# A weight exchange on TensorE, half of the v loads on another engine's queue, and a new order on GpSimd, in a windowed attention and gated convolution kernel

## The chip, the cores and the metric

The kernel runs on one core of one Trainium2 chip. The metric is the device time of one execution in microseconds (us). A single-core run is called slow here when it lies over 1.5% above the fastest run of the same kernel; the comparisons of times below use the other, fast, runs.

## The reference

There are 8 batches, 8 heads, 576 positions and 64 channels per head. Heads 0 to 3 see a plain window of 32 positions, heads 4 to 7 a window dilated by 4. The output of the attention, 512 channels wide, is the input of a causal gated convolution unit.

```python
def _attn_ref(q, k, v):
    window, dilation, scale = 32, 4, 1.0 / np.sqrt(D)
    scores = scale * np.matmul(q, k.transpose(0, 1, 3, 2))
    mask_plain = (rel >= 0) & (rel < window)
    mask_dil = (rel >= 0) & (rel < window * dilation) & (rel % dilation == 0)
    ...                                   # masked softmax over the keys
    return np.matmul(attn, v)

def _moe_ref(x, w_val, conv_w, w_out):
    for k in range(5):
        gate_pre += conv_w[k] * xp[:, k:k + S, :]      # causal, per channel
    gate = 1.0 / (1.0 + np.exp(-gate_pre))
    return (gate * (x @ w_val)) @ w_out
```

## The kernel before

The work is cut into 32 iterations: four per batch, each of two heads (128 channels). Iterations 0 and 1 of a batch are plain heads, 2 and 3 dilated ones. A *group* `g` is four heads of a batch, so group 2b is the plain half of batch b and group 2b + 1 the dilated one. The names that matter:

- `k_nat`, `q_nat`, `qk_rest`: loaded k and q; `k_b`, `q_b`: the same converted to bf16 for plain heads.
- `vPst`, `v_st`: loaded plain and dilated v; `vP`, `vA`: converted by GpSimd. `vPst` has two halves: partitions 0 to 63 (z = 0) and 64 to 127 (z = 1, the "upper half"), each with a load of its own.
- `w_out_b`: the output weights. Output tiles of one parity read them as they are, the others read `w_out_s`, in which the two halves of 64 rows are exchanged.

```python
def load_v(g, a=0, e=4, eng=nc.sync):
    ...
    if not dil:
        per = NB // 2
        dst = vPst[b % NVP]
        for z in range(2):
            ...
            eng.dma_start(out=dst[D * z:D * z + D, first:e * per, :], in_=...)

def swap_out():                       # the exchange of the halves, by DMA
    for h in range(2):
        nc.gpsimd.dma_start(out=w_out_s[D * h:D * h + D], in_=w_out_b[D - D * h:2 * D - D * h])

# (cut) before the loop
    make_mask_d()
    make_perm()
    prep_v(0)                         # GpSimd: v of iteration 0 to bf16
    for i in range(NP):
        # (cut) loads of the groups ahead, all on SyncE's queue
        if i + 1 < NP:
            prep_v(i + 1)
        # (cut) early k/q conversions
        if i == 3:
            load_weight(w_out_b, moe_w_out)
        if i == 5:
            swap_out()
        g2 = g + 2
        if 2 < g2 < 2 * B and g2 % 2 == 0:
            cast(g2, "k" if a == 0 else "q", 0, nc.gpsimd)
            cast(g2, "k" if a == 0 else "q", 2, nc.gpsimd)
        scores(i, 0)                  # TensorE, then exp on ScalarE
        scores(i, 1)
        if i == 0:
            cast(0, "k", 2, nc.scalar)
            cast(0, "q", 2, nc.scalar)
        run_conv(i - 1)               # TensorE, then the gate on ScalarE
        # (cut) masks, transposes of the next pair
        attn_v(i, 0)                  # attention products, read vP or vA
        attn_v(i, 1)
        normalize(i)
        # (cut) the value products and output tiles of the batch before
```

The softmax here doesn't subtract the row's maximum and nothing guards it: scores larger than these inputs give would overflow.

Of the kernel before, what the change touches and what calls it, by code (L numbers as in the profile page):

```python
# [23 lines left out]
def kernel(  # L24
# [47 lines left out]


    ident = consts.tile([128, 128], BF16, name="ident")
    perm = consts.tile([96, 96], BF16, name="perm")
    ident5 = consts.tile([8, 8], FP32, name="ident5")
    mask_p = consts.tile([128, NB, 96], BF16, name="mask_p")
# [27 lines left out]
    def bank():  # L105
        return ps_one.tile([128, 512], FP32, name="ps_bank")
# [16 lines left out]
    def load_rest(g, name, eng):  # L123
# [14 lines left out]
        else:  # L138
# [2 lines left out]
                in_=bass.AP(tensor=src.tensor, offset=off,  # L141
                            ap=[[2 * D, 2 * TR], [S * D, 4], [1, 2 * D]]))

    def load_v(g, a=0, e=4, eng=nc.sync):
        b, dil = g // 2, g % 2
        t = grp_tiles.setdefault(g, {})
        if not dil:


            per = NB // 2  # L150
            dst = vPst[b % NVP]
            for z in range(2):
                first = a * per
                if b == 0 and a == 0 and z == 0:
                    eng.dma_start(
                        out=dst[16:D, 0, :],
                        in_=v[0, 0, 0:96, :].rearrange("(p j) d -> p (j d)", j=2))
                    first = 1
                eng.dma_start(
                    out=dst[D * z:D * z + D, first:e * per, :],  # L160
                    in_=bass.AP(
                        tensor=v.tensor,
                        offset=v.offset + (b * H * S + 192 * first + 96 * z - 32) * D,
                        ap=[[2 * D, D], [192 * D, e * per - first], [1, 2 * D]]))
        else:
            if "vst" not in t:
                t["vst"] = vst_pool.tile([128, 4, DIL * D], FP32, name="v_st")
                t["vBst"] = vst_pool.tile([128, 4, 2, D], FP32, name="vB_st")
            eng.dma_start(
                out=t["vst"][:, a:e, :],  # L170
                in_=v[b, 4 + a:4 + e, 0:RM, :].rearrange("h (p r) d -> p h (r d)", r=DIL))
            eng.dma_start(
                out=t["vBst"][:, a:e].rearrange("p h j d -> p h (j d)"),
                in_=v[b, 4 + a:4 + e, DIL * TB:S, :].rearrange("h (p j) d -> p h (j d)", j=2))
# [8 lines left out]
    def cast(g, name, a, eng):  # L183

        t = grp_tiles[g]
        if name + "b" not in t:
            t[name + "b"] = qb_pool.tile([128, DIL, 4, D], BF16, name=f"{name}_b")
        dst = t[name + "b"][:, :, a:a + 2, :]
        src = t[name][:, a:a + 2, :].rearrange("p h (r d) -> p r h d", r=DIL)
        if eng is nc.scalar:  # L190
            nc.scalar.copy(out=dst, in_=src)
        else:
            eng.tensor_copy(dst, src)  # L193

    def prep_v(i):
        b, c, dil, g, a = pair_info(i)
        t = grp_tiles[g]
        e = a + 2
        if not dil:
            nc.gpsimd.tensor_copy(  # L200
                vPs[b % NVP][:, a:e, :, 0:D],
                vPst[b % NVP][:, a * NB // 2:e * NB // 2, :].rearrange(
                    "p (h u) (j d) -> p h (u j) d", u=NB // 2, j=2))
        else:
            nc.gpsimd.tensor_copy(
                vAs[b % NVD][:, a:e, :, 0:D],
                t["vst"][:, a:e, :].rearrange("p h (r d) -> p h r d", r=DIL))
            nc.gpsimd.tensor_copy(
                vBs[b % NVD][:, a:e, :, 0:D], t["vBst"][:, a:e, :, :])
# [6 lines left out]
    def load_pair(g, a):  # L216
        load_main(g, "k", a, a + 2, nc.sync)
        load_main(g, "q", a, a + 2, nc.sync)
        if a == 0:
            load_rest(g, "k", nc.sync)  # L220
            load_rest(g, "q", nc.sync)
        load_v(g, a, a + 2)
# [5 lines left out]
    load_rest(0, "k", nc.sync)  # L228
    load_rest(0, "q", nc.scalar)
    load_v(0, 0, 2)  # L230
    nc.scalar.dma_start(out=conv_nat, in_=moe_conv_w)
    nc.scalar.activation(out=warm_in, in_=warm_in, func=AF.Exp, scale=1.0)
    load_main(0, "k", 2, 4, nc.sync)
    load_main(0, "q", 2, 4, nc.sync)
    load_v(0, 2, 4)
    load_pair(1, 0)
    load_pair(1, 2)
    nc.vector.memset(junk, 1.0)
# [5 lines left out]
        base=0, pattern=[[-1, 128]], channel_multiplier=1,  # L244
    )
    nc.vector.tensor_tensor(out=ident_h, in0=ident[:, 0:D], in1=ident[:, D:2 * D], op=ALU.add)
    nc.gpsimd.memset(ident5, 0.0)
    nc.gpsimd.affine_select(
        out=ident5, in_=ident5, compare_op=ALU.not_equal, fill=1.0,
# [50 lines left out]
    def make_mask_d():  # L300
        band(mask_d[:, 0:TM], [[1, TM]], 0)
        nc.gpsimd.tensor_copy(mask_d[:, TM:2 * TM], mask_d[:, 0:TM])

        mb = mask_d[:, 2 * TM:HB].rearrange("p (w t) -> p w t", w=2)
        nc.gpsimd.memset(mb, 1.0)
        for (lo, up) in ((True, 0), (False, 0)):
            sg = 1 if lo else -1
            base = 2 * (TM - TB) if lo else 2 * (window - 1) - 2 * (TM - TB)
            nc.gpsimd.affine_select(
                out=mb, in_=mb, compare_op=ALU.is_ge, fill=0.0, base=base,  # L310
                pattern=[[sg, 2], [2 * sg, TR]], channel_multiplier=-sg)
        nc.gpsimd.iota(par_i, pattern=[[1, 2]], base=1, channel_multiplier=1)
# [19 lines left out]
    def make_conv_diag(c):  # L332
        nc.vector.tensor_tensor(
            out=conv_diag[:, c, :, :],
            in0=ident_h[:, None, :].to_broadcast([128, K, D]),
            in1=conv_w_sb[:, c, :, None].to_broadcast([128, K, D]),
            op=ALU.mult)

    def swap_val():
        x, y = (w.rearrange("p m (c h d) -> p (m c) h d", h=2, d=D) for w in (w_val_b, w_val_s))  # L340
        for h in range(2):
            nc.gpsimd.tensor_copy(y[:, :, h, :], x[:, :, 1 - h, :])

    def swap_out():
        for h in range(2):
            nc.gpsimd.dma_start(out=w_out_s[D * h:D * h + D], in_=w_out_b[D - D * h:2 * D - D * h])

    def load_weight(dst, src):
        nc.gpsimd.dma_start(out=dst, in_=src.rearrange("(c p) n -> p c n", p=128))
# [315 lines left out]
    setup_conv_w()  # L665
    make_conv_diag(0)
    make_conv_diag(1)
    make_mask_d()
    make_perm()
    prep_v(0)  # L670
    for i in range(NP):
        b, c, dil, g, a = pair_info(i)
        if i == 0:
            load_pair(2, 0)
        elif i == 1:
            load_pair(2, 2)
        elif i == 2:
            load_pair(3, 0)
        elif i == 3:
            load_pair(3, 2)  # L680
            load_group(4)
        if c % 2 == 0 and 5 <= g + 3 < 2 * B:
            load_group(g + 3)
        if i + 1 < NP:
            prep_v(i + 1)
        if i == 1:
            load_weight(w_val_b, moe_w_val)
        if i == 2:
            for name in ("k", "q"):
                cast(2, name, 0, nc.gpsimd)  # L690
        if i == 3:
            load_weight(w_out_b, moe_w_out)
            for name in ("k", "q"):
                cast(2, name, 2, nc.gpsimd)
        if i == 4:
            swap_val()
        if i == 5:
            swap_out()
        g2 = g + 2
        if 2 < g2 < 2 * B and g2 % 2 == 0:  # L700
            cast(g2, "k" if a == 0 else "q", 0, nc.gpsimd)
            cast(g2, "k" if a == 0 else "q", 2, nc.gpsimd)
        scores(i, 0)
        scores(i, 1)
        if i == 0:
            cast(0, "k", 2, nc.scalar)
            cast(0, "q", 2, nc.scalar)
        run_conv(i - 1)
        apply_mask(i, 0)
        if i > 0:  # L710
            after_x(i - 1)
        if 1 < i < NCH:
            next_pair(i)
        if i >= EARLY and g + 1 < 2 * B:
            trans_main(g + 1, "k" if a == 0 else "q")
        apply_mask(i, 1)
        if 0 < i < 3:
            make_conv_diag(i + 1)
        if i < NCH:
            warm(3 if i == 0 else 2)  # L720
        elif c == 0 and outs:
            run_out()
        elif vals:
            run_val()
        attn_v(i, 0)
        attn_v(i, 1)
        normalize(i)
        if i == 1 or NCH <= i < EARLY:
            next_pair(i)
        if i == EARLY - 1:  # L730
            trans_main(g + 1, "k")
        if i == 0:
            next_pair(0)
            finish_mask_d()
        elif i >= EARLY - 1 and a == 0 and g + 1 < 2 * B:
            trans_rest(g + 1)
        if i < NCH - 1:
            warm(2)
        if c == 0 and vals:
            run_val()  # L740
        for _ in range((2 if len(outs) > 2 else 1) - (c == 0 and i > NCH)):
            if outs:
                run_out()
        if vals:
            run_val()
# [39 lines left out]
```

## Time and profile before

| | kernel before |
|---|---|
| time, median of the runs beside the changed kernel | 183.33 us (182.02 to 184.41, 4 runs) |
| span of the profiled execution | 183.2 us (that run took 185.49 us as a whole, 2 us above the median and 1.9% above the fastest run, so slow by the rule above; its granted clock, 0.963, is like that of the fast ones) |
| TensorE busy | 87% of the span |
| longest wait of TensorE | 5.2 us, for `w_out_s` |

The views are read in the prediction below: the page's busy times and slices, the chain of work that ended last, the stretches around the hole. One more view of the kernel before is needed later, ScalarE's timeline in iteration 0. The columns of an engine's timeline are the start, the busy time, engine, line, operation, output and input; in brackets stands the idle time ahead of it and what ended it.

```profile
7.05 1.19 ACT L456 ACTIVATE et<-ps_sc 128x576 bf16<-128x576 f32 x2 [0.85 <-PE ps_sc L436]
8.13 0.62 ACT L191 CAST k_b<-k_nat 128x512 bf16<-128x512 f32 x1
9.48 0.62 ACT L191 CAST q_b<-q_nat 128x512 bf16<-128x512 f32 x1 [0.73 <-DMA q_nat<-in_q_dram]
```

After the two exponentials ScalarE converts k at 8.13 us and q at 9.48 us. TensorE needs both to go on to iteration 1.

### The profile page before, as it was taken

To read this page: it belongs to the slowest core of one execution; us is meant where nothing else is said; L and a number is where in the kernel's file an instruction comes from. 1 tells how busy PE (TensorE), PEld (TensorE's weight loads), DVE (VectorE), ACT (ScalarE), POOL (GpSimd) and SP (SyncE) were. 2 spreads that over 40 slices of the span, in tenths; PEclk is the share of its full clock that TensorE was granted. 3 is DMA by queue.
4 is the path that set the end of the run, shared out by engine and by line. 5 is a ranking of instruction groups with operands and counts; after the bars stand their busy time and mean duration, and the time that the engine had idled before them with its cause. 6 is when DMAs were issued, how large, how long until landed. Compare 5 with 4: busy or idle time off the path is not lost.

```text
span 183.2 us, 6768 instructions
## 1 busy us (share of the span) xinstructions
PE 158.7 (87%) x2799; PEld 108.8 (59%) x2827; DVE 120.2 (66%) x292; ACT 115.9 (63%) x217; POOL 59.2 (32%) x118
## 2 busy tenths in 40 slices
PE   6768878979259999999996999999999999999990
PEld 2445556656137667667774776777677767665540
DVE  4647667855404988688775766976797869773320
ACT  3625764759227677777874788778877786564440
POOL 7857166065302730850093028300750400000000
PEclk9957999999957999999999999999999999999999
DMA  5999999999999999999999999999999322224354
GB/s 149 249 300 326 236 263 260 357 197 193 206 338 245 214 319 362 231 334 334 291 222 300 296 291 221 307 309 290 185 333 343 106 61 61 61 57 106 104 166 145
DMA packets 51688, 42.91 MB, mean 234 GB/s; under 512 B 6997, under 2 KB 46917, under 8 KB 51658
## 3 DMA queue, kind: packets, MB, share of 16 engines
q1 hardware_dynamic: 49888, 40.57, 84.1%
q0 software_dynamic: 1216, 1.57, 4.9%
q8 instruction: 22, 0.36, 0.9%
q10 hardware_dynamic: 554, 0.34, 0.6%
q14 instruction: 8, 0.07, 0.1%
HBM read 33.56 MB, written 9.44 MB: 235 GB/s over the span
## 4 chain that ended last, share of the span: by engine, by line
PE 72%; DVE 7%; POOL 6%; DMA 6%; issue 4%; ACT 2%; POOLq 0%; ACTq 0%
PE ps_bank L599 17%; PE ps_bank L583 14%; PE ps_bank L566 12%; PE ps_bank L365 7%; DMA w_out_s<-w_out_b 6%; PE ps_sc L479 5%; PE ps_sc L436 3%; PE ps_sc L493 3%; PE ps_sc L453 3%; DVE et L465 3%; PE ps_bank L520 3%; PE ps_bank L533 2%; DVE xn L508 2%; PE ps_bank L527 2%; DVE xT L535 1%
## 5 line engine op out<-in xcount | busy, mean ns | idle before, releaser
L456 ACT ACTIVATE et<-ps_sc 128x576 bf16<-128x576 f32 x64 | 38.5, 648 | 13.8 <-PE ps_sc L436 9.9
L604 ACT ACTIVATE osb<-ps_bank 128x512 f32<-128x512 f32 x36 | 21.9, 608 | 32.7 <-PE ps_bank L599 26.1
L589 DVE SCALAR_TENSOR_TENSOR y<-gate,ps_bank 128x288 bf16<-128x288 bf16 x64 | 28.3, 450 | 11.8 <-PE ps_bank L583 9.6
L508 DVE TENSOR_TENSOR xn<-ps_sc,rec 96x768 bf16<-96x768 f32 (+1 forms) x32 | 30.6, 955 | 1.1
L566 PE MATMUL ps_bank<-xT,conv_diag 64*64 64x288 bf16 (+1 forms) x768 | 27.9, 270 | 0.0
L193 POOL CAST k_b<-k_nat 128x512 bf16<-128x512 f32 x14 | 9.2, 679 | 53.9 <-DMA k_nat<-in_k_dram 18.5
L465 DVE TENSOR_TENSOR et<-et,mask_p 128x576 bf16<-128x576 bf16 x32 | 17.4, 547 | 10.8 <-ACT et L456 10.8
L575 ACT ACTIVATE gate<-ps_bank 128x288 bf16<-128x288 f32 x64 | 23.0, 422 | 2.0 <-PE ps_bank L566 1.7
L599 PE MATMUL ps_bank<-w_out_s,y 128*128 128x512 bf16 x59 | 18.4, 394 | 6.1 <-DMA w_out_s<-w_out_b 5.2
L599 PEld LDWEIGHTS <-y 128*128 128x128 bf16 x144 | 12.8, 99 | 17.3 <-issue 6.6
L566 PEld LDWEIGHTS <-conv_diag 64*64 64x64 bf16 x768 | 19.3, 108 | 3.0 <-DVE qB L420 1.0
L583 PE MATMUL ps_bank<-xT,w_val_s 128*128 128x288 bf16 x128 | 20.7, 285 | 0.0
L583 PE MATMUL ps_bank<-xT,w_val_b 128*128 128x288 bf16 x128 | 19.9, 286 | 0.4 <-DVE xT L535 0.4
L465 DVE TENSOR_TENSOR et<-et,mask_d 128x576 bf16<-128x576 bf16 x32 | 15.5, 486 | 6.6 <-ACT et L456 6.4
L535 DVE COPY xT<-ps_bank 128x576 bf16<-128x576 bf16 x32 | 14.6, 456 | 7.4 <-PE ps_bank L533 4.4
L200 POOL CAST vP<-vPst 128x768 bf16<-128x768 f32 x16 | 13.1, 841 | 18.5 <-DMA vPst<-in_v_dram 16.7
L599 PE MATMUL ps_bank<-w_out_b,y 128*128 128x512 bf16 x58 | 17.7, 379 | 0.7
L503 DVE RECIPROCAL rec<-ps_sc 96x12 f32<-96x12 f32 (+1 forms) x32 | 7.4, 231 | 13.8 <-PE ps_sc L479 11.1
L583 PEld LDWEIGHTS <-w_val_s 128*128 128x128 bf16 x128 | 12.1, 97 | 5.6
L479 PE MATMUL ps_sc<-vP,et 64*128 64x65 bf16 x384 | 10.2, 197 | 5.4 <-POOL vP L200 2.9
L479 PEld LDWEIGHTS <-et 64*128 64x128 bf16 x384 | 7.7, 98 | 12.0 <-issue 5.7
L583 PEld LDWEIGHTS <-w_val_b 128*128 128x128 bf16 x128 | 11.7, 98 | 3.6 <-issue 0.2
(93 smaller groups left out, 239.2 us busy)
## 6 DMA issues: line engine op xcount, KB each, us to landing
k_nat<-in_k_dram SPq DMA_DIRECT2D x12, 512.0 KB, 6.5
q_nat<-in_q_dram SPq DMA_DIRECT2D x12, 512.0 KB, 8.0
vPst<-in_v_dram SPq DMA_DIRECT2D x12, 384.0 KB, 8.4
v_st<-in_v_dram SPq DMA_DIRECT2D x6, 512.0 KB, 6.4
k_nat<-in_k_dram SPq DMA_DIRECT2D x8, 256.0 KB, 4.5
out_dram<-osb SPq DMA_DIRECT2D x8, 256.0 KB, 6.4
q_nat<-in_q_dram SPq DMA_DIRECT2D x7, 256.0 KB, 5.0
out_dram<-osb SPq DMA_DIRECT2D x8, 224.0 KB, 5.2
```

The source lines that it names most:

```text
L200: nc.gpsimd.tensor_copy(vPs[b % NVP][:, a:e, :, 0:D], vPst[b % NVP][:, a * NB // 2:e * NB // 2, :].rearrange("p (h u) (j d) -> p h (u j) d ...
L456: nc.scalar.activation(out=e3, in_=ps[:, :, 0:HB], func=AF.Exp, scale=scale)
L465: nc.vector.tensor_tensor(out=e3, in0=e3, in1=m, op=ALU.mult)
L479: nc.tensor.matmul(out=ps[:, z, x * AVS:x * AVS + D + 1], lhsT=et[D * z:D * z + D, h2, col:col + 128], rhs=vPs[b % NVP][D * z:D * z + D, a ...
L508: nc.vector.tensor_tensor(out=dst, in0=av[:, :, :, 0:D], in1=rec[0:R, :, :, None].to_broadcast([R, 2, 6, D]), op=ALU.mult)
L535: nc.vector.tensor_copy(xTs[b % NXT][:, c, :, 2:], pr)
L566: nc.tensor.matmul(out=pss[G][D * hp:D * hp + D, o * T:(o + n) * T], lhsT=conv_diag[D * h:D * h + D, c, K - 1 - m, :], rhs=xt[D * h:D * h ...
L575: nc.scalar.activation(out=gate, in_=pss[G][:, 0:HB], func=AF.Tanh, scale=0.5)
L583: nc.tensor.matmul(out=ps[:, 0:HB], lhsT=w[:, mc, c * 128:(c + 1) * 128], rhs=xt[:, mc, 2 * G:2 * G + 2, 2:], start=(mc == 0), stop=(mc == ...
L589: nc.vector.scalar_tensor_tensor(out=y_half[G][:, c, b * HB:(b + 1) * HB], in0=gates.pop((b, c, G)), scalar=1.0, in1=ps[:, 0:HB], op0=ALU. ...
L599: nc.tensor.matmul(out=ps, lhsT=y_half[G][:, c, 128 * n:128 * n + 128], rhs=w[:, c, :], start=(c == 0), stop=(c == NCH - 1),)
L604: nc.scalar.mul(out=osb, in_=ps, mul=0.5)
```

## The change

The intent is to end two waits of TensorE and to shorten the loads' way. **One**: the exchanged weights are made by TensorE, as a product with an exchanged identity matrix, instead of by two copies that take over 10 us. **Two**: the upper half of plain v is issued by ScalarE, so that SyncE has fewer issues to make and v arrives sooner. **Three**: GpSimd converts v of iteration 0 ahead of making the masks, and around iterations 4 to 6 v ahead of q and k; from iteration 8 on it is the other way round.

```diff
+    ident_x = consts.tile([128, 128], BF16, name="ident_x")   # identity, halves exchanged
@@ load_v: the loop over z becomes a function of its own
+    def load_v_half(g, z, a, e, eng): ...
     def load_v(g, a=0, e=4, eng=nc.sync):
         if not dil:
-            for z in range(2): ...
+            load_v_half(g, 0, a, e, eng)
@@ ahead of the loop
     load_v(0, 0, 2)
+    load_v_half(0, 1, 0, 2, nc.scalar)
     ...
     load_v(0, 2, 4)
+    load_v_half(0, 1, 2, 4, nc.scalar)
@@
-    def swap_out():
-        for h in range(2):
-            nc.gpsimd.dma_start(out=w_out_s[D * h:D * h + D], in_=w_out_b[D - D * h:2 * D - D * h])
+    def swap_out(m, eng):
+        ps = bank()
+        nc.tensor.matmul(out=ps, lhsT=ident_x, rhs=w_out_b[:, m, :], start=True, stop=True)
+        ...                                   # evicted by ScalarE (three) and VectorE (one)
@@
+    prep_v(0)
     make_mask_d()
     make_perm()
-    prep_v(0)
@@ in the loop
-        if i + 1 < NP:
+        if i < 4:
             prep_v(i + 1)
         if i == 4:
             swap_val()
+            prep_v(5)
+            prep_v(6)
+        g2 = g + 2
         if i == 5:
-            swap_out()
-        g2 = g + 2
-        if 2 < g2 < 2 * B and g2 % 2 == 0:
+            prep_v(7)
+            for z in (0, 2):
+                cast(4, "k", z, nc.gpsimd)
+        elif i == 6:
+            for z in (0, 2):
+                cast(4, "q", z, nc.gpsimd)
+        elif 4 < g2 < 2 * B and g2 % 2 == 0:
             cast(g2, "k" if a == 0 else "q", 0, nc.gpsimd)
             cast(g2, "k" if a == 0 else "q", 2, nc.gpsimd)
+        if 7 <= i < NP - 1:
+            prep_v(i + 1)
         scores(i, 0)
         scores(i, 1)
+        if i == 0:
+            load_v_half(2, 1, 0, 2, nc.scalar)
+        elif i == 1:
+            load_v_half(2, 1, 2, 4, nc.scalar)
+        elif i == 3:
+            load_v_half(4, 1, 0, 4, nc.scalar)
+        elif c % 2 == 0 and 5 <= g + 3 < 2 * B and (g + 3) % 2 == 0:
+            load_v_half(g + 3, 1, 0, 4, nc.scalar)
         if i == 0:
             cast(0, "k", 2, nc.scalar)
             cast(0, "q", 2, nc.scalar)
@@ in iteration 5, around normalize(i)
+            swap_out(0, nc.scalar); swap_out(1, nc.scalar)
+            swap_out(2, nc.scalar); swap_out(3, nc.vector)
```

More of the change, by code (lines that the diff above doesn't have):

```diff
@@ L142, in load_rest, with load_v_half @@
                             ap=[[2 * D, 2 * TR], [S * D, 4], [1, 2 * D]]))
+    def load_v_half(g, z, a, e, eng):
+        b, per = g // 2, NB // 2
+        first, dst = a * per, vPst[b % NVP]
+        if b == 0 and a == 0 and z == 0:
+            eng.dma_start(
+                out=dst[16:D, 0, :],
+                in_=v[0, 0, 0:96, :].rearrange("(p j) d -> p (j d)", j=2))
+            first = 1
+        eng.dma_start(
+            out=dst[D * z:D * z + D, first:e * per, :],
+            in_=bass.AP(
+                tensor=v.tensor,
+                offset=v.offset + (b * H * S + 192 * first + 96 * z - 32) * D,
+                ap=[[2 * D, D], [192 * D, e * per - first], [1, 2 * D]]))
     def load_v(g, a=0, e=4, eng=nc.sync):
@@ L147, in load_v @@
         if not dil:
-            per = NB // 2
-            dst = vPst[b % NVP]
-            for z in range(2):
-                first = a * per
-                if b == 0 and a == 0 and z == 0:
-                    eng.dma_start(
-                        out=dst[16:D, 0, :],
-                        in_=v[0, 0, 0:96, :].rearrange("(p j) d -> p (j d)", j=2))
-                    first = 1
-                eng.dma_start(
-                    out=dst[D * z:D * z + D, first:e * per, :],
-                    in_=bass.AP(
-                        tensor=v.tensor,
-                        offset=v.offset + (b * H * S + 192 * first + 96 * z - 32) * D,
-                        ap=[[2 * D, D], [192 * D, e * per - first], [1, 2 * D]]))
+            load_v_half(g, 0, a, e, eng)
         else:
@@ L246 @@
     nc.vector.tensor_tensor(out=ident_h, in0=ident[:, 0:D], in1=ident[:, D:2 * D], op=ALU.add)
+    for h in range(2):
+        nc.vector.tensor_copy(ident_x[:, D * h:D * h + D], ident[:, D - D * h:2 * D - D * h])
     nc.gpsimd.memset(ident5, 0.0)
@@ L342, in swap_val @@
             nc.gpsimd.tensor_copy(y[:, :, h, :], x[:, :, 1 - h, :])
-    def swap_out():
-        for h in range(2):
-            nc.gpsimd.dma_start(out=w_out_s[D * h:D * h + D], in_=w_out_b[D - D * h:2 * D - D * h])
+    def swap_out(m, eng):
+        ps = bank()
+        nc.tensor.matmul(out=ps, lhsT=ident_x, rhs=w_out_b[:, m, :], start=True, stop=True)
+        if eng is nc.scalar:
+            nc.scalar.copy(out=w_out_s[:, m, :], in_=ps)
+        else:
+            eng.tensor_copy(w_out_s[:, m, :], ps)
     def load_weight(dst, src):
@@ L726 @@
         attn_v(i, 1)
+        if i == 5:
+            swap_out(0, nc.scalar)
+            swap_out(1, nc.scalar)
         normalize(i)
+        if i == 5:
+            swap_out(2, nc.scalar)
+            swap_out(3, nc.vector)
         if i == 1 or NCH <= i < EARLY:
```

## The prediction

> **What bounds the kernel now.** I read the page first, its slices and the chain of work that ended last:
>
> ```profile
> PE 158.7 (87%) x2799; PEld 108.8 (59%) x2827; DVE 120.2 (66%) x292; ACT 115.9 (63%) x217; POOL 59.2 (32%) x118
> ...
> PE   6768878979259999999996999999999999999990
> ...
> PEclk9957999999957999999999999999999999999999
> DMA  5999999999999999999999999999999322224354
> ...
> PE 72%; DVE 7%; POOL 6%; DMA 6%; issue 4%; ACT 2%; POOLq 0%; ACTq 0%
> ```
>
> One slice is 4.58 us. From slice 12 on (55 us) TensorE is full to the end, so there it sets the time; the DMA engines are full until slice 30 (142 us). Before that TensorE has one hole, in slices 10 and 11, and its granted clock is low just after it. The same chain in order of time, then the stretches around the hole (columns: stretch, busy us of PE, PEld, DVE, ACT, POOL, clock, DMA share, GB/s):
>
> ```profile
> 38.19 1.27 POOL k_b L193 x2
> 39.46 0.78 POOL vA L205
> 40.59 0.48 POOL w_out_s L346
> 41.06 10.91 DMA w_out_s<-w_out_b
> 52.11 0.58 PE ps_bank L599
> ```
>
> ```profile
> 41.00:46.80 5.80, 5.36 (x93) 4.07 (x90) 3.71 (x10) 5.27 (x10) 2.65 (x6) 1.00 1.13 191
> 46.80:52.10 5.30, 0.11 (x4) 0.02 (x1) 1.34 (x3) 0.29 (x1) 1.60 (x2) 0.85 1.11 242
> 52.10:58.20 6.10, 5.82 (x68) 3.56 (x70) 1.28 (x3) 3.15 (x6) 0.00 (x0) 0.57 1.12 318
> ```
>
> GpSimd works in order. Its k conversion waits for k of group 4 until 38.19, the copies that make the half-exchanged w_out stand behind it, they go out at 40.54 and land about 10.6 us later, and the first output tile that reads them stops TensorE for 5.2 us (46.8 to 52.1) and leaves it at a clock of 0.57 for 6 us. A smaller hole is at the start: the first attention product waits 2.94 us for vP, because GpSimd makes mask_d and perm (6.93 to 10.03) before that conversion.
>
> **What the Trainium skill says.** "TensorE: Matmul & The Clock Gate", Part 1 (the HAM clock gate): TensorE falls to half rate after an idle window of about 3.4 us and needs about as long again to recover. The trace agrees in kind: 0.57 after 5.2 us idle, and 0.50 in 10 to 15 us after the 2.94 us wait. "DMA: Bandwidth & Descriptors", Issuing engines are not separate DMA queues: queues of different engines share the 16 DMA engines, so a second queue saves only issue time. The trace agrees: the v halves cost SyncE 0.64 us of issue each, while the DMA share is over 1.0 in every stretch from 5 to 100 us. Same page, Queues, rings and completion order: each DMA engine takes turns between queues. So a v half on the ScalarE queue goes past what waits on SyncE's queue; no run shows it yet. "Trainium Kernel Development and Optimization", Key Constraints: GpSimd cannot access PSUM; hence the four exchanged blocks must leave PSUM by ScalarE and VectorE, as the diff has them.
>
> **Part by part.**
> (1) Exchange on TensorE. Removed: two copies of 256 KB, the wait of 5.2 us, and the slow clock behind it. Size of the latter: from the first score product of iteration 8 to its attention product took 53.90 to 58.22 = 4.32 us; the same stretch of iteration 12 at full clock took 72.95 to 75.83 = 2.88. That is 1.4; the output tile before it (52.11 to 53.90 = 1.79, against 0.9 at 71.50 to 72.36) gives 0.9. Together 5.2 + 2.3 = **7.5 us** if nothing else stops TensorE. The copies' DMA work goes too: 23.6% of 11.2 us = 2.6 us on their queue (DMA view, 41 to 52.2). Added: four 512-column products at about 0.38 us (row of L599), three ScalarE evictions of 0.6 us (row of L604) and one on VectorE. They stand in iteration 5 (about 34 us), where TensorE next waits for loads (below), so I count 0.
> (2) prep_v(0) ahead of the masks. vP can be made at 7.0 to 7.8 instead of 10.03 to 10.84; the masked scores are ready at 9.03. Gain 10.89 - 9.0 = 1.9 us, and about 1 us of clock. But in iteration 6 the transposes of group 4 need k and q rest rows, whose q part lands at 42.43, and TensorE already waited 0.4 us for it. A start 2 to 3 us earlier only waits longer there: 0 at the end.
> (3) Upper v halves on ScalarE. Packets take 42 to 49 ns each of an engine (queue share x 16 x stretch / packets: 0.908 x 13 us x 16 / 4521 = 42 ns), so a half of 768 packets is 768 x 42 / 16 = 2.0 us of DMA. Issued earlier, it pushes all loads of the SyncE queue behind it back by 2.0 us; against that, SyncE is rid of two issues of 0.64 at the start (1.3 us earlier). Rest q of group 4 then lands at 42.43 + 2.0 - 1.3 = 43.1. ScalarE pays some ten issues of 0.64 us at 63% busy, mostly in its idle time.
> (4) Order on GpSimd. In iterations 4 to 6 v goes ahead of k/q, which ends a 1.31 us wait for vA at 39 us (hidden by the wait at 43.1). But from iteration 8 on the diff puts the k/q conversions **ahead** of prep_v(i + 1); before they came after it:
>
> ```profile
> 47.13 1.60 POOL L200 CAST vP<-vPst 128x768 bf16<-128x768 f32 x2 [3.48 <-DMA vPst<-in_v_dram]
> 58.43 1.17 POOL L193 CAST k_b<-k_nat 128x512 bf16<-128x512 f32 x2 [9.70 <-PE ps_bank L599]
> ```
>
> ```profile
> 62.51 0.63 PE L479 MATMUL ps_sc<-vP,et 64*128 64x65 bf16 x24
> ```
>
> The vP of iteration 9 was made at 47.9. Now it waits for k of group 6, which landed at 58.23 (issued 49.03, 9.2 us). In the new kernel that is 58.23 - 2.6 (copies gone) + 2.0 (the v half of group 6 now ahead) - 1.3 = 56.3; plus two k casts 1.2 and one vP 0.83: vP ready at 58.3. TensorE would want it at 46.8 + 0.65 (rest q) + 10.4 (52.11 to 62.51) - 2.3 (clock) = 55.5. So it waits 2.8 us and starts iteration 9 at 58.3 instead of 62.5: **4.2 us** is left of 7.5. Check of the next gates, with the landing times of before: vA of iteration 10 behind the q cast, ready 59.7 + 2.2 = 61.9, wanted at 66.64 - 4.2 = 62.4: fits. Iteration 13: k landed 74.08, vP at 76.5, wanted at 80.12 - 4.2 = 75.9, but k lands about 1.9 earlier: fits. Iteration 17: 93.6 against 97.75 - 4.2 = 93.5: just fits. Behind that TensorE is full to the end, so the gain stays.
>
> Sum: 183.4 - 4.2 = 179.2; I say **179.0 us**, as the gate at 58.3 is the shakiest number and full gain is larger than no gain is likely.
>
> **The rivals.**
> (a) The GpSimd order costs nothing, because k of group 6 lands by 53.5 or so (two queues being served faster than one, loads of the first 50 us ahead). For: SyncE's queue is backed up there (issues of 1.8 to 2.9 us instead of 0.45), and fewer descriptors stand in it. Against: time per packet hardly changes with queues or sizes. Then the gain is 7 to 7.5: about 176.
> (b) The loads bind more than I think: the v halves delay q of groups 4 and 6 by the full 2.0 and no 1.3 is won, TensorE stands over 3 us in iteration 6 and again in 9, and its clock falls again (1 to 2 us). For: DMA full throughout, and a 2.94 us wait was enough at the start. Gain 1 to 2.5: 181 to 182.4.
> (c) ScalarE becomes the bound, since a DMA issue sits in its order between the exponentials and the gates. For: it is 70 to 80% busy in full stretches. Against: 0.64 us once in four iterations of 4.4 us. At most 1 us in all.
>
> **Range and chances.** The middle is 4.2 gained, (a) gives 7.5 and (b) 1 to 2.5. Range 175.8 to 181.9. 2% is 3.7 us, or 179.8: the middle is only just beyond it. (a) with nearly a third and the upper half of the middle make 0.6 for faster; same 0.37; slower 0.03, since every added cost lies beside waits.
>
> **What would show it.** Right: no wait of an output tile for w_out_s; PEclk full around 50 to 55 us unless a new hole is there; no wait of 2.9 us at the start, yet TensorE near its old time at iteration 6, waiting for qk_rest; in iteration 9 a wait of TensorE on vP of 1.5 to 3 us, right after the k casts of group 6; from there as full as before. Wrong: no wait on vP at iteration 9 (then 176), or waits for vP at iterations 13 and 17 as well, or a clock that falls twice (then over 181); or TensorE well over 1 us ahead of its old times already at iteration 7, which would mean that the loads do not gate there.

## The result, and the profile after

| | before | after |
|---|---|---|
| median of the runs | 183.33 us | 189.8 us (188.77 to 190.41, 4 runs, all fast) |
| ratio | | 1.035, 95% interval 1.026 to 1.044: slower |
| span of the profiled execution | 183.2 us | 187.4 us |

A ratio here and below is the mean time of one kernel's fast runs over that of the other's of the same rounds, so it is not quite the ratio of the medians quoted beside it.

The page of the changed kernel (busy times, the slices of TensorE, its clock and the DMA engines, the chain's shares by engine):

```profile
PE 164.5 (88%) x2831; PEld 110.0 (59%) x2831; DVE 120.6 (64%) x295; ACT 117.0 (62%) x220; POOL 57.3 (31%) x116
...
PE   6536983898999589999999999999999999999990
...
PEclk9855798559999999999999999999999999999997
DMA  5999999999999999688899999989989322123354
...
PE 71%; DMA 15%; DVE 6%; ACT 3%; issue 2%; ACTq 1%; POOL 0%
```

ScalarE's busy time has hardly changed (115.9 to 117.0 us). TensorE's rose by 5.8 us, beside a longer time at half clock: 24 us (7.6 to 21.3 and 31.5 to 41.8), against 14 us before (9.6 to 16.4 and 50.5 to 57.4). And TensorE has new holes in slices 1 to 3 (5 to 19 us) and in slice 6 (28 to 33 us), and the DMA share of the chain went from 6% to 15%. The chain in order of time says where (start, length, what):

```profile
12.21 4.68 DMA v_st<-in_v_dram
...
16.91 9.31 DMA k_nat<-in_k_dram
...
26.23 4.90 DMA v_st<-in_v_dram
...
31.19 0.62 POOL vA L207
31.81 0.04 ACTq L155
...
31.90 0.42 ACT gate L585
...
32.36 0.37 PE ps_bank L410 x2
```

Up to 31 us the chain is one load after another, and from there it goes over a DMA issue on ScalarE (`ACTq L155`, the upper half of v) to a gate and to TensorE. ScalarE's timeline of the changed kernel shows that issue twice, in iteration 0 and in iteration 3:

```profile
8.70 1.19 ACT L466 ACTIVATE et<-ps_sc 128x576 bf16<-128x576 f32 x2 [1.03 <-PE ps_sc L446]
14.19 0.60 ACTq L155 DMA_DIRECT2D vPst<-in_v_dram  x1
14.84 0.62 ACT L193 CAST k_b<-k_nat 128x512 bf16<-128x512 f32 x1 [4.94 <-DMA v_st<-in_v_dram]
```

```profile
27.37 0.65 ACT L466 ACTIVATE et<-ps_sc 128x576 bf16<-128x576 f32 x1 [0.31 <-PE ps_sc L463]
31.23 0.62 ACTq L155 DMA_DIRECT2D vPst<-in_v_dram  x1
31.90 0.71 ACT L585 ACTIVATE gate<-ps_bank 128x288 bf16<-128x288 f32 x2 [3.88 <-POOL vA L207]
```

The issue takes 0.60 us as predicted. But ScalarE is done with its exponentials at 9.89 us and the issue begins at 14.19, 4.3 us later; the k conversion, which stood at 8.13 us before, comes behind it at 14.84. In iteration 3 it is 28.02 to 31.23, 3.2 us. The second releaser is named wrongly: vA of line 207 runs from 31.19 to 31.81, so it cannot release what begins at 31.23.

What does the issue wait for? The program as compiled lists the semaphores. These are lines of ScalarE's program of the changed kernel (the number counts its instructions), and two of SyncE's; the list is not a profile:

```
ScalarE
11 L466 Activation et0_104<-ps_sc_290 128x576 [waits PE_49]
12 L155 DMACopy vPst1_107<-in_v_dram 64x6x128 [waits DMAHW0_49]
13 L193 TensorCopy k_b_220<-k_nat_129 128x4x128
...
31 L155 DMACopy vPst0_106<-in_v_dram 64x12x128 [waits DMAHW4_49,DMAHW3_49,Pool_49]
32 L585 Activation gate_636<-ps_bank_610 128x288 [waits PE_49]
SyncE
12 L171 DMACopy v_st_152<-in_v_dram 128x2x256 [waits DMAHW0_49]
30 L171 DMACopy v_st_473<-in_v_dram 128x2x256 [waits DMAHW4_49]
```

The loads and stores of SyncE's and ScalarE's queues share eight completion semaphores, DMAHW0 to DMAHW7, in rotation over both queues. Each further issue waits until the transfer that had the semaphore before it, eight issues back, has **landed**. For ScalarE's instruction 12 that is SyncE's instruction 12, a `v_st` load. The view of that tile in the changed kernel (its issue, who waited for it, and its time from issue to landing):

```profile
L171 SPq DMA_DIRECT2D v_st<-in_v_dram x1: 592/592/592, 9.3 to 9.3; - x1
...
  ACT k_b L193: 4.9, 1
...
DMA to landing us min/median/max: 4.9/4.9/4.9
```

Issued at 9.27 us, landed 4.9 us later at 14.17; ScalarE's issue begins at 14.19. For iteration 3: issued 26.23, landed 31.13, ScalarE's issue at 31.23. A further issue at 5.92 us waits in the same way for the rest rows of k.

Two statements of the Trainium skill make this worse than it looks. "DMA: Bandwidth & Descriptors", Anatomy of one DMA — SWDGE (gpsimd) path: "any semaphore wait happens on the issuing sequencer before dispatch". It is written of GpSimd's path; the trace agrees for ScalarE's. And "PSUM — Partial Sum Buffer", Engine vs sequencer instructions: the queues of ScalarE, VectorE and GpSimd are strict FIFO, which agrees with the k conversion moving from 8.13 to 14.84 us: its k, issued at 4.59 us, landed 4.2 us later, so it was there by 8.8. SyncE waits in this way as well, but it computes nothing. Behind ScalarE's issue stand the conversions and gates that TensorE needs. TensorE's timeline of the changed kernel:

```profile
10.22 1.02 PE L489 MATMUL ps_sc<-vP,et 64*128 64x65 bf16 x24
15.51 0.61 PE L375 MATMUL ps_bank<-ident,k_b 128*128 128x128 bf16 x4 [4.27 <-ACT k_b L193]
...
32.36 0.37 PE L410 MATMUL ps_bank<-ident,qk_rest 128*128 128x128 bf16 x2 [2.95 <-ACT gate L585]
...
56.82 1.02 PE L609 MATMUL ps_bank<-w_out_s,y 128*128 128x512 bf16 x4
```

A third, earlier wait of 2.14 us belongs to the issue at 5.92 us, which pushed a q conversion from 4.65 to 6.57. The stretches of the changed kernel (columns as in the prediction) show what follows each hole:

```profile
15.50:20.50 5.00, 4.88 (x66) 2.71 (x66) 3.30 (x8) 2.25 (x4) 2.89 (x5) 0.50 1.23 250
29.40:32.40 3.00, 0.05 (x2) 0.04 (x1) 0.00 (x0) 0.50 (x2) 2.24 (x3) 0.86 1.19 227
32.40:40.50 8.10, 7.29 (x106) 5.15 (x106) 4.40 (x12) 3.34 (x8) 1.41 (x3) 0.50 1.14 308
```

The clock is at half in the stretch behind each hole. At the start it had already fallen at 7.6 us, after the wait of 2.14 us and before that of 4.27, and stayed at half until 21.3; the second time it fell at 31.5, within the wait of 2.95 us, and was at half until 41.8. In the last line of TensorE's timeline an output tile on `w_out_s` starts with no wait at all: the wait of 5.2 us is gone, as predicted.

### The profile page after: what moved, and what is told of

It reads as the page before. It is cut to its first block, busy times and chain, and to the rows that moved or that the text cites. A ratio compares the mean times of both kernels' runs of the same rounds, so it can differ in the third digit from the quotient of the medians.

```text
span 187.4 us, 6792 instructions
## 1 busy us (share of the span) xinstructions
PE 164.5 (88%) x2831; PEld 110.0 (59%) x2831; DVE 120.6 (64%) x295; ACT 117.0 (62%) x220; POOL 57.3 (31%) x116
## 4 chain that ended last, share of the span: by engine, by line
PE 71%; DMA 15%; DVE 6%; ACT 3%; issue 2%; ACTq 1%; POOL 0%
PE ps_bank L609 17%; PE ps_bank L593 17%; PE ps_bank L576 12%; DMA k_nat<-in_k_dram 8%; PE ps_bank L375 5%; DMA v_st<-in_v_dram 5%; PE ps_sc L489 4%; PE ps_sc L446 3%; PE ps_sc L463 3%; DMA vPst<-in_v_dram 3%; PE ps_bank L530 3%; PE ps_sc L503 2%; DVE xT L545 2%; PE ps_bank L543 2%; PE ps_bank L537 2%
## 5 line engine op out<-in xcount | busy, mean ns | idle before, releaser
L195 POOL CAST k_b<-k_nat 128x512 bf16<-128x512 f32 x14 | 8.5, 630 | 60.4 <-DMA k_nat<-in_k_dram 25.1
L593 PE MATMUL ps_bank<-xT,w_val_b 128*128 128x288 bf16 x128 | 21.1, 297 | 2.3 <-issue 2.1
L475 DVE TENSOR_TENSOR et<-et,mask_d 128x576 bf16<-128x576 bf16 x32 | 14.9, 466 | 7.0 <-ACT et L466 6.8
L475 DVE TENSOR_TENSOR et<-et,mask_p 128x576 bf16<-128x576 bf16 x32 | 15.7, 493 | 4.7 <-ACT et L466 4.7
L609 PE MATMUL ps_bank<-w_out_b,y 128*128 128x512 bf16 x72 | 18.4, 378 | 0.3
L593 PEld LDWEIGHTS <-w_val_b 128*128 128x128 bf16 x128 | 12.2, 102 | 6.5 <-issue 2.6
L207 POOL CAST vA<-v_st 128x512 bf16<-128x512 f32 x16 | 9.9, 616 | 9.2 <-DMA v_st<-in_v_dram 9.2
```

Of the source, the lines that this page charges most:

```text
L475: nc.vector.tensor_tensor(out=e3, in0=e3, in1=m, op=ALU.mult)
L593: nc.tensor.matmul(out=ps[:, 0:HB], lhsT=w[:, mc, c * 128:(c + 1) * 128], rhs=xt[:, mc, 2 * G:2 * G + 2, 2:], start=(mc == 0), stop=(mc == ...
L609: nc.tensor.matmul(out=ps, lhsT=y_half[G][:, c, 128 * n:128 * n + 128], rhs=w[:, c, :], start=(c == 0), stop=(c == NCH - 1),)
```

## The experiments

The theory: issues on ScalarE wait for the landing of the load eight before, and what stands behind them starves TensorE. Rivals: the moved loads themselves, arriving in another order, delay others; the new GpSimd order costs the time; the exchange on TensorE does not pay. The kernels called `e1` to `e4` ran beside the kernel before on one chip, as did `e6` to `e9`; `e10` to `e13` ran on another, beside the kernel before again. Across chips I compare ratios to the kernel before, not times. All results were correct.

Start of TensorE's attention products, and the span, of the profiled runs, in us. All are fast except that of the kernel before (see above): the spans of its fast runs beside e1 to e4 were 179.7 to 182.3, so differences from its 183.2 are 1 to 3 us too large.

| kernel | iteration 0 | 1 | 4 | 8 | span |
|---|---|---|---|---|---|
| before | 10.89 | 15.56 | 29.67 | 58.22 | 183.2 |
| after | 10.22 | 19.50 | 38.94 | 60.90 | 187.4 |
| e1, halves back on SyncE | 9.24 | 13.44 | 27.25 | 51.73 | 176.2 |
| e3, exchange only | 10.83 | 15.06 | 29.05 | 50.31 | 176.3 |
| e6, v first from iteration 8 on | 8.72 | 12.78 | 26.64 | 52.66 | 177.0 |
| e7, only late halves on ScalarE | 9.00 | 13.11 | 27.82 | 58.96 | 184.7 |
| e8, only early halves on ScalarE | 10.09 | 19.16 | 37.99 | 59.91 | 183.4 |
| e9, halves on GpSimd's queue | 10.53 | 14.96 | 29.50 | 53.62 | 180.0 |
| e10, standing still in 0 and 3 | 8.72 | 18.50 | 38.63 | 59.50 | 185.2 |
| e12, standing still in 6 | 8.81 | 13.34 | 27.14 | 59.55 | 183.8 |
| e11, w_out loaded earlier | 9.05 | 13.16 | 27.80 | 51.80 | 175.7 |
| e13, exchange and first v | 8.81 | 13.09 | 26.90 | 50.80 | 176.4 |

From iteration 8 to the end every one of them takes 123.5 to 126.5 us. So a difference at the end above 3 us is one made ahead of iteration 8.

### e1: the halves back on SyncE, the rest of the change kept

```diff
         if not dil:
-            load_v_half(g, 0, a, e, eng)
+            for z in range(2):
+                load_v_half(g, z, a, e, eng)
-    load_v_half(..., nc.scalar)          # all six calls gone
```

> The changed kernel with only the upper v halves put back on SyncE's queue (in their old places). Theory Q (ScalarE's in-order stream stands still while its v loads wait for an earlier load to land: 4.3 us in iteration 0 and 3.2 us in iteration 3, and TensorE with it): ScalarE's holes of 4.3 and 3.2 us go, TensorE's holes of 4.27 us at 11 us and 2.95 us at 29 us go, and the kernel is faster than the one before: 176 to 180 us. Rival O (the conversions of k and q standing ahead of v on GpSimd cost the time): still 186 us or more, with a TensorE wait for vP in iteration 9. Rival X (the exchange on TensorE brings nothing and costs TensorE and ScalarE time): 183 us or more.

Measured: 178.55 us (177.62 to 179.87), ratio 0.973 (0.965 to 0.981). Set against the 1.035 of the changed kernel, the halves on ScalarE cost 1.035 / 0.973 = 1.064, some 11 us; the spans say 187.4 - 176.2 = 11.2. This one part makes the gain a loss. By the table 9.2 of the 11.2 us are made before iteration 8 (60.90 - 51.73). The other 2.0 come after it, where the changed kernel has a wait of 2.07 us, at 61.8 us, for which the profile shows no releaser; so up to 2 us of the 11 may have another cause. Two smaller waits of TensorE remain in e1:

```profile
34.39 1.02 PE L351 MATMUL ps_bank<-w_out_b,ident_x 128*128 128x512 bf16 x2 [1.96 <-DMA w_out_b<-in_moe_w_out_dram]
...
57.11 0.55 PE L488 MATMUL ps_sc<-vP,et 64*128 64x65 bf16 x24 [1.01 <-POOL vP L203]
```

The first is the exchange product waiting for its weights in iteration 5. The second is the vP of iteration 9 behind the k conversions of group 6, the gate that the prediction named.

### e2: the halves alone on ScalarE, on the kernel before

```diff
         if not dil:
-            for z in range(2): ...
+            load_v_half(g, 0, a, e, eng)
+    load_v_half(..., nc.scalar)          # the same six calls as in the change
```

> The kernel before with only the upper v halves moved to ScalarE's queue. Theory Q: slower than before, 187 to 193 us, with the same holes of ScalarE at iterations 0 and 3, and the wait for w_out_s of some us still there (shorter, as TensorE comes later). Rivals O and X: about 183 us, within 1%.

Measured: 191.29 us (189.82 to 193.7), ratio 1.039 (1.030 to 1.049): slower. The halves do the harm alone, with neither of the other parts. Here they cost about 7 us and not 11, so the parts do not add up. The expectation that some of the wait for `w_out_s` would be left was a miss, and this is a reason. The profiled run is a slow one, so no duration of it is compared; but it shows the first output tile on `w_out_s` starting without any wait:

```profile
58.20 1.02 PE L602 MATMUL ps_bank<-w_out_s,y 128*128 128x512 bf16 x3
```

The two copies had landed by 54.04 us. TensorE came so late that the 5.2 us wait of the kernel before is hidden behind the new ones.

### e3: the exchange alone

```diff
-            swap_out()                    # two copies by DMA
+            swap_out(0, nc.scalar) ...    # four products with ident_x in iteration 5
```

> The kernel before with only the half-exchanged w_out made on TensorE. Theory Q, and the prediction's part 1: the 5.2 us wait and the slow clock behind it go, 176 to 179 us, unless loads gate TensorE next (then a new wait on qk_rest or k_nat at 48 to 55 us, and 179 to 181). Rival X: 183 us or more.

Measured: 177.97 us (176.77 to 180.81), ratio 0.967 (0.958 to 0.976): faster. By the fast runs of the same rounds the exchange is worth 183.61 - 177.57 = 6.0 us. The spans say 183.2 - 176.3 = 6.9, with the long profiled run of the kernel before; in the table it all comes between iterations 4 and 8 (29.05 to 50.31, against 29.67 to 58.22). No kernel tried here has a lower ratio.

### e4: the GpSimd order alone

```diff
+    prep_v(0)                             # ahead of the masks
...
+        # the conversions of iterations 4 and later in the order of the change
```

> The kernel before with only the new order on GpSimd (first v conversion ahead of the masks, v of iterations 5 to 7 ahead of k and q, then k and q ahead of v); the copies for w_out stay, now issued right after the conversions of iteration 6's v, ahead of the k conversion of group 4, so about 36 instead of 40.5 us. Theory Q: the copies land by 46 to 47 us, the wait of 5.2 us nearly goes, 177 to 180 us; a wait for vP in iteration 9 of up to 3 us would be the prediction's gate. Rival O: 186 us or more.

Measured: 181.2 us (179.88 to 183.15), ratio 0.985 (0.975 to 0.994). That is over the 177 to 180 expected, and far from rival O's 186: the new order does not make the loss. Its gain of 1.5% on the kernel before is not the order's alone, since the edit also brings the copies for `w_out_s` forward. In its profile, of a slow run, they are issued at 33.9 us instead of 40.5 and landed by 44.1, and no product waits for `w_out_s`. The changed kernel has no such copies, so nothing of this gain can be had there.

### e6: e1 with v ahead of the conversions from iteration 8 on

```diff
-        if i < 4:
+        if i < 4 or 7 <= i < NP - 1:
             prep_v(i + 1)
...
-        if 7 <= i < NP - 1:
-            prep_v(i + 1)
```

> The kernel with the upper v halves back on SyncE's queue (178.6 us), and from iteration 7 on the old order on GpSimd, v ahead of k and q. The prediction's gate (vP of iteration 9 waits behind the k conversion of group 6) showed there as a wait of 1.0 us: if that is all that order costs, 0.5 to 1.5 us faster, 177 to 178 us, with no wait for vP in iteration 9. If the order is worth more at the later batches: under 176.5. If it is worth nothing: 178.5.

Measured: 179.53 us (178.32 to 181.45), ratio 0.977 (0.966 to 0.988), against 0.973 of e1; 177 to 178 us had been expected. The 1.01 us wait on vP in iteration 9 is gone, but the time is not better; iteration 8 is reached 0.9 us later than in e1. The gate of the prediction is real and not worth a measurable amount.

### e7: only the halves of the later batches on ScalarE

```diff
-            load_v_half(g, 0, a, e, eng)
+            for z in range(2 if g <= 4 else 1):
+                load_v_half(g, z, a, e, eng)
...
-        if i == 0: ... elif i == 1: ... elif i == 3: ...       # the early calls gone
+        if i > 3 and c % 2 == 0 and 5 <= g + 3 < 2 * B and (g + 3) % 2 == 0:
             load_v_half(g + 3, 1, 0, 4, nc.scalar)
```

> The changed kernel with the upper v halves of batches 0 to 2 (iterations up to 3) back on SyncE's queue, those of batches 3 to 7 still on ScalarE's. Theory Q says that the holes of 4.3 and 3.2 us, both early, make nearly all of the loss: 179 to 182 us (178.6 plus about 0.4 us in each of five batches, as the trace of the changed kernel shows there, plus at most one wait of some us in iteration 6). If the issues cost mostly by their number: 186 us or more.

Measured: 186.28 us (185.12 to 188.74), ratio 1.013 (1.005 to 1.021), so 4% above e1 and well over the 179 to 182 us expected. By its number it fits the rival that the issues cost by their count (186 or more), but the trace shows nearly the whole loss at one place, the issue in iteration 6 (ScalarE's timeline of e7, then TensorE's):

```profile
37.52 1.19 ACT L465 ACTIVATE et<-ps_sc 128x576 bf16<-128x576 f32 x2
47.62 0.62 ACTq L155 DMA_DIRECT2D vPst<-in_v_dram  x1
48.29 0.71 ACT L584 ACTIVATE gate<-ps_bank 128x288 bf16<-128x288 f32 x2 [9.58 <-issue]
```

```profile
48.76 1.01 PE L374 MATMUL ps_bank<-ident,k_b 128*128 128x128 bf16 x8 [7.89 <-ACT gate L584]
```

The load eight before is k of group 5, issued at 37.70 and landed 9.5 us later, at 47.20. ScalarE stands for 9.58 us, TensorE for 7.89. In the changed kernel this same issue stood at 49.23 us and waited for nothing, since that kernel came there 11.5 us later (its exponentials begin at 49.02 us, those of e7 at 37.52) and k of group 5 had landed at about 47.6. That is why e7 and e8 do not add up: the wait in iteration 6 is hidden behind the earlier ones. From iteration 9 to the end e7 falls only 0.9 us further behind e1 (7.6 to 8.5 us), with four more such issues: late, an issue on ScalarE is about as cheap as the prediction had it.

### e8: only the early halves on ScalarE

```diff
+            for z in range(1 if g <= 4 else 2):
+                load_v_half(g, z, a, e, eng)
...
-        elif c % 2 == 0 and 5 <= g + 3 < 2 * B and (g + 3) % 2 == 0:
-            load_v_half(g + 3, 1, 0, 4, nc.scalar)
```

> The changed kernel with the upper v halves of batches 3 to 7 back on SyncE's queue, the first five loads still on ScalarE's. Theory Q: still slow, 186 to 189 us, with the same two holes of ScalarE. If the issues cost mostly by their number or in the later batches: 180 to 183.

Measured: 185.72 us (184.56 to 186.41), ratio 1.011 (1.004 to 1.019); 186 to 189 had been expected. Its start times follow those of the changed kernel (19.16 at iteration 1, 37.99 at iteration 4). The spans give 183.4 - 176.2 = 7.2 us over e1; e7 gives 8.5 (7.7 by the medians); both together cost 11.2.

### e9: the same halves at the same places, on GpSimd's queue

```diff
-            load_v_half(2, 1, 0, 2, nc.scalar)
+            load_v_half(2, 1, 0, 2, nc.gpsimd)      # and so in all six calls
```

> The changed kernel with the same loads at the same places of the program, but issued from GpSimd's queue. Its loads wait for no landing of a load on the hardware queues, so nothing of ScalarE's work stands behind such a wait; the DMA engines still serve these loads ahead of those of SyncE's queue. Theory Q: ScalarE's holes go, 177 to 181 us. Rival L (the early v halves take the DMA engines from k and q, which TensorE needs first): as slow as the changed kernel, 186 to 190, with TensorE waiting for k, q or rest rows in iterations 0 to 6.

The compiled program shows that loads from GpSimd's queue have completion semaphores of another family and wait for no load eight before. Measured: 181.15 us (180.34 to 183.13), ratio 0.986 (0.978 to 0.994), just over the 177 to 181 us expected. ScalarE's timeline of e9, iteration 0 and then iteration 3:

```profile
9.86 0.62 ACT L193 CAST k_b<-k_nat 128x512 bf16<-128x512 f32 x1 [0.34 <-DMA k_nat<-in_k_dram]
...
28.36 0.71 ACT L585 ACTIVATE gate<-ps_bank 128x288 bf16<-128x288 f32 x2
```

No standing still at either place. The v halves go ahead of SyncE's queue here too, and no later than in the changed kernel (four of them are issued at 13.75, 17.05, 29.47 and 44.84 us, there at 14.19, 19.68, 31.23 and 49.23), so the order of the loads is not what cost the 11 us. About 2.6 us over e1 remain. Part of it is a wait of 1.78 us for vP in iteration 9, where e1 had 1.01, and GpSimd issues transfers ahead of its first conversion of v; how the rest divides is not settled.

### e10 and e12: no load moved, ScalarE only made to stand still

Both are e1, with a copy of one number by ScalarE at the place of the issue. The copy reads the load that the issue had waited for, so ScalarE must wait for its landing; nothing else changes.

```diff
         scores(i, 1)
+        if i == 0:                            # e10
+            nc.scalar.copy(out=seen, in_=grp_tiles[1]['vst'][0:1, 0, 0:1])
+        if i == 3:                            # e10
+            nc.scalar.copy(out=seen, in_=grp_tiles[3]['vst'][0:1, 0, 0:1])
+        if i == 6:                            # e12 instead
+            nc.scalar.copy(out=seen, in_=grp_tiles[5]['k'][0:1, 0, 0:1])
```

> No load moved: the kernel with all v halves on SyncE's queue (178.6 us), plus two copies of one element by ScalarE, in the places of the program where the changed kernel's loads stood in iterations 0 and 3, each reading a v tile whose landing those loads had to wait for (the compiled listing shows the same semaphores). If standing still behind a landing is the cause by itself: ScalarE idle for about 4 us and 3 us there, and 184 to 187 us, as with the early loads on ScalarE (185.7). If the moved loads cost by taking the DMA engines or by their issue time: within 1 us of 178.6.

> As the run before, but with a single such copy in iteration 6, reading k of group 5, whose landing (47.2 to 47.5 us) the load there waited for. Theory: ScalarE idle from about 38.5 to 47.5 us, TensorE for 5 to 8 us, 184.5 to 187 us, as with only the later loads on ScalarE (186.3). Otherwise within 1 us of 178.6.

Measured: e10 185.21 us (184.5 to 187.03), ratio 1.016 (1.008 to 1.025), as slow as e8 (1.011), which moved the loads. e12: 185.78 us (183.18 to 187.31), two of its four runs slow and no ratio given; its two fast runs, 185.55 and 183.18, are 1.3% apart and on average 1.0% above the fast runs of the kernel before there (184.37 against 182.62), where e7 has 1.3%. So for e12 the table and the trace say more than the time. ScalarE's timeline of e10, then of e12:

```profile
13.98 0.19 ACT L725 COPY seen<-v_st 1x1 f32<-1x1 f32 x1 [6.20 <-DMA v_st<-in_v_dram]
...
31.18 0.19 ACT L727 COPY seen<-v_st 1x1 f32<-1x1 f32 x1 [4.34 <-DMA v_st<-in_v_dram]
```

```profile
47.04 0.19 ACT L725 COPY seen<-k_nat 1x1 f32<-1x1 f32 x1 [5.96 <-DMA k_nat<-in_k_dram]
```

ScalarE stands still for 6.20 and 4.34 us in e10, more than the 4 and 3 expected and the 4.3 and 3.2 of the changed kernel, because it comes to the first place earlier (its exponentials end at 7.78 us, not 9.89). TensorE waits 5.27 and 4.20 us behind it. In e12 ScalarE stands for 5.96 us (about 9 expected) and TensorE waits 4.79 (5 to 8 expected). The copies take 0.19 us of ScalarE; the landings they wait for fall where the issues began in the changed kernel (14.19 and 31.23) and in e7 (47.62). In the table e10 goes with e8 and e12 with e7, from iteration to iteration. Standing still behind the landing is enough to make the loss, with no load moved and no issue on ScalarE.

### e11 and e13: can more be had?

e11 is e6 with `w_out_b` loaded in iteration 2 instead of 3, against the 1.96 us wait seen in e1. e13 is e3 with the conversion of the first v ahead of the masks, and no other change of order.

```diff
         if i == 2:                            # e11
+            load_weight(w_out_b, moe_w_out)
...
         if i == 3:
-            load_weight(w_out_b, moe_w_out)
```

```diff
+    prep_v(0)                                 # e13
     make_mask_d()
     make_perm()
-    prep_v(0)
```

> The kernel with v halves on SyncE's queue and v always ahead on GpSimd, w_out now loaded one iteration earlier, so that the exchange in iteration 5 does not wait for it (it waited 2.5 us at 32 us). The prediction said that an early start is lost at the rest rows of q of group 4, which land at about 41.8 us. If so: TensorE waits there instead, 177 to 179.5 us. If the early start of about 2 us can be kept: 175 to 177.

> The kernel before with two parts only: the exchange on TensorE, and the first v conversion ahead of the masks. The exchange alone gave 178.0. The prediction counts 0 for the first v conversion: 177 to 178.5. If its 1.9 us are kept: 175.5 to 176.5.

Measured: e11 179.0 us (176.6 to 182.85), ratio 0.970 (0.963 to 0.978); e13 178.56 us (176.97 to 179.32), ratio 0.977 (0.970 to 0.985). Neither is clearly apart from e3's 0.967. In e11 the wait for `w_out_b` is gone and smaller ones, for vP and `q_b` of group 2 (0.77 and 1.20 us), stand in its place. In e13 the start is 2 us earlier than in e3 up to iteration 4 (26.90 against 29.05), and by iteration 8 nothing of it is left (50.80 against 50.31): TensorE waits 1.38 us for `w_out_b` in iteration 5, and for loads.

## Why the prediction was wrong

**What bounds the kernel**: right. The hole of 5.2 us was on the path, and removing it alone moved the end.

**Part (1), the exchange, 7.5 us if nothing else stops TensorE**: right, the size too large: 6.0 us by the fast runs of before and e3 (ratio 0.967), 6.9 by the spans. From 45 to 55 us the clock of e3 is 1.00, and the products cost nothing visible.

**Part (2), an earlier first v, 0 at the end**: right in the sum (e13 against e3), not by the gate that was named. In e1 and e3 no product waited for the rest rows of q of group 4; what was gained at the start went in waits for `w_out_b` in iteration 5, and in e11 for data of group 2.

**Part (3), the step that failed.** It said: "ScalarE pays some ten issues of 0.64 us at 63% busy, mostly in its idle time." The 0.64 us was taken from the issues' duration in the trace of before, where it is right at the median (up to 1.8 us), and it held after the change (0.60 and 0.62). What was left out is the wait **ahead** of an issue. SyncE's issues waited for landings in the trace of before too (6.3 us in nine waits ahead of the rest rows of q and k, for `vPst`), but there no computing stands behind them. On ScalarE they came to 4.3 and 3.2 us, with TensorE's holes of 4.27 and 2.95 us behind them, one of 2.14 us behind the earlier issue at 5.92 us, and its clock at half for 13.7 and for 10.3 us around them. Together 11 us (e1 against after; up to 2 of them open), instead of 0; e10 makes the early part of the loss, and e12 that of e7, with no load moved. The same term fooled rival (c), which saw the issue in ScalarE's order as the danger, but put it at "at most 1 us in all". Two of the signs of being wrong came true in the changed kernel, both by this cause and not by the one they stood for: the clock fell twice, and iteration 9 had no wait on vP.

**Part (4), the GpSimd order, 2.8 us of wait in iteration 9**: the gate was named rightly and was too large: 1.01 us in e1, since k of group 6 landed at 54.6 us there and not at 56.3; of the prediction's sum for it, the 2.0 us for a half of v ahead on another queue does not apply to e1. In the changed kernel it did not show at all, since TensorE came late. Removing it gained nothing measurable (e6).

**Two readings that turned on nothing.** "Packets take 42 to 49 ns each" holds for the stretch from 13 to 26 us that it was worked out from; the stretch of the copies, 41 to 52.2 us, gives 0.864 x 11.2 us x 16 / 2357 = 66 ns a packet. And the DMA share from 5 to 10 us is 1.00, not over it.

**The sum.** With parts (1), (2) and (4) alone e1 gives 178.55 us, close to the 179.0 predicted for everything. The predicted value holds for the kernel without part (3). That it holds so closely is partly luck: the exchange was worth 6.0 us instead of 7.5, and the gate took 1.0 instead of 2.8. And e3, with part (1) alone, is as fast.

**What stays open.** The changed kernel has a wait of 2.07 us at 61.8 us for which the profile shows no releaser; the kernel before has one of 1.69 at 98 us, e7 one of 1.37. They vary from kernel to kernel. In each of these three a packet of 16 KB on the DMA queue that the profile calls "instruction" ends 1.3 to 1.5 us before the wait does (62.41 and 63.86 us; 98.40 and 99.71; 59.78 and 61.22). That would fit a wait for instructions, but it is not shown: such packets come all through a run, mostly without a wait. Together with e9's rest these waits are too small to change the verdict.

## What to carry to other kernels

A DMA issue put on a computing engine must be judged by what it waits for, not by how long it takes: in its program it stands in line, and if it must wait for an older transfer to land, all the work behind it waits too. Read the semaphores that the compiled issue waits on and compare them with the landing times in the trace; a copy of one number that reads the awaited load shows the price without moving anything. Test the parts of a change one by one, because here a gain of 6 to 7 us and a loss of 11 us were in the same diff, and two losses of 7.2 and 8.5 us (e8 and e7) together cost 11.

## What the Trainium skill lacked or had wrong

- "DMA: Bandwidth & Descriptors", Issuing engines are not separate DMA queues, says that issuing on several engines only saves issue time. The page's section on GpSimd's path has the wait on the issuing sequencer. What both lack is the price on an engine that computes: 1.064 between the changed kernel and e1, about 11 us (2.0 of them open), with waits of 4.3 and 3.2 us ahead of issues of 0.6 us (and 9.6 us in e7).
- No page of the skill tells that in the compiled program the transfers of SyncE and ScalarE share eight completion semaphores in rotation, so that an issue waits for the landing of the one eight before: landed 14.17, issued 14.19; landed 31.13, issued 31.23; landed 47.20, issued 47.62. Issues on GpSimd's queue had no such wait (e9).
- "TensorE: Matmul & The Clock Gate", Part 1, has the clock fall after an idle window of about 3.4 us. Here it was at half 1.6 us into the 2.94 us wait of the kernel before (wait from 7.95 us, half from 9.6) and 2.1 us into the 2.95 us wait of the changed one (wait from 29.41, half from 31.5). These do not give a shorter window as a rule: the 2.07 us wait at 61.8 us left the clock at 1.00, while a wait of 1.96 us in e1 was followed by 0.51 from 34.4 to 37.9 us. The recovery, which the prediction quotes from there as about as long again, took longer in the changed kernel: TensorE worked again from 15.5 and from 32.4 us, and the clock was back at 21.3 and at 41.8, after 5.8 and 9.4 us.
